# First feed-forward product of the last batch and of all last tokens by Strassen's scheme, seven products of 256x128x512 for eight

## The chip, the cores and the metric

The kernel runs on one core of one Trainium2 chip. The metric is the device time of one execution in microseconds (us), median of three runs. Five engines work side by side and meet at semaphores: PE (the matrix engine, with PEld for its weight loads), DVE (vector), ACT (scalar), POOL and SP (which issues most transfers).

## What is computed

Block-causal attention over 8 batches, 8 heads, 576 tokens, 64 columns a head, then a feed-forward layer with a maximum over three products, all in float32:

```python
B, H, S, D = attn_out.shape
x = attn_out.transpose(0, 2, 1, 3).reshape(B * S, H * D)      # 4608 x 512
h = np.maximum(np.maximum(x @ w1, x @ w2), x @ w3)            # 4608 x 768
return (h @ w_out).astype(np.float32)                         # 4608 x 512
```

## The kernel before

Channels (512, in four tiles of 128 that belong to the four pairs of heads) lie on the partitions and tokens on the free axis. Each float32 operand of the feed-forward products is split into a float32r high part and a float32r rest, and a product is three matmuls: high by high, high by rest, rest by high (`Chunk.product`, L1381). The split of an activation is a cast on ACT (`high`, printed as L286) and a subtraction on POOL (`low`, L291); L286, L288 and L291 are lines of the helpers `copy` and `minus`, which many steps share.

A batch has 576 tokens: 512 go through the feed-forward layer as one `Chunk` (L1317) of 512 columns. The last 64 tokens of each batch are stored to a scratch tensor `rest` in HBM (`Pair.save`, L1236); after the last batch the 8 x 64 of them are loaded back and split (`Rest`, L1261) and make one more chunk of 512 columns. A `Chunk` makes 6 tiles f of 128 hidden columns; for each, the three weights i and the four channel tiles c give 12 steps of three matmuls of 128x128 by 128x512, so 216 matmuls, into a PSUM bank `pm` for each (f, i). ACT copies the bank of i = 0 to SBUF (`m`), DVE takes the maximum with the other two (`most`, L1400), ACT and POOL split the result into `hh`, `hl`. Then four output tiles tt of 128 tokens take 6 x 3 matmuls each (`project`, L1415), 72 in all; ACT copies the bank (`get`) and SP sends it off (`put`, L1430).

The order on every engine is written by a planner (`in_order`, L65). Each step is a job with a cost for each engine, a rank, the jobs that it waits for and the buffers ("slots") that it takes and gives. The planner plays the program through with these costs; a free engine takes the ready job of the lowest rank (`NOW` is the lowest of all), and the order that comes out is the order in which the instructions stand in the engines' queues. The products of the chunk of batch b-1 fill PE between the attention of batch b, so that after the attention of batch 7 there remain, in this order: the rest of batch 6's products, its projections, the products and projections of batch 7's 512 tokens, and the products and projections of the last tokens (L1476 to L1490).

The weights are split once at the start and stay in SBUF as `wh`, `wl` (tiles `w0` to `w17`).

Of the kernel before, what the change touches and what calls it, by code (L numbers as in the profile page):

```python
# [9 lines left out]
F32 = mybir.dt.float32  # L10
# [24 lines left out]
LOAD = 520.0  # L35
# [115 lines left out]
def pe(*cols, least=128):  # L151
    return sum(max(n, least) / 2.4 + 13.5 for n in cols)


def dve(n, fast=False):
    return (70.0 if fast else 72.0) + n / (1.92 if fast else 0.96)


def act(n, psum=True):
    return (55.0 if psum else 95.0) + n / 1.2  # L160


def pool(n):
    return 120.0 + 2.2 * n
# [3 lines left out]
def kernel(  # L168
# [40 lines left out]

    slots = dict(  # L210
        sb=5, sb5=4, scores=4, pm=3, stat=2, stat4=2, p0=2, p1=2, p2=2, p3=2, p4=1,
        x32=2 * XB, x=NP, m=3, qn=2, kn=2, vn=2, kq=2, q8=1, pz=2, pt=2,
    )
    for f in range(NF):
        slots[f"hh{f}"] = slots[f"wo{f}"] = 1
# [58 lines left out]
    def job(cost, rank, call, *args, after=(), take=(), give=(), lasts=0.0, moved=0.0, behind=None, alone=("POOL",)):  # L274
        j = Job(cost, rank, lambda eng: call(eng, *args), after, take, give, lasts, moved, behind, alone)

        j.late = 500.0 if call.__name__ in ("qk4", "block", "pv") else 250.0
        jobs.append(j)
        return j

    def join(after, give):
        return job({}, 0, lambda eng: None, after=after, give=give)

    def copy(eng, dst, src):
        if eng == "ACT":
            nc.scalar.copy(dst, src)  # L286
        else:
            nc.vector.tensor_copy(dst, src)  # L288

    def minus(eng, dst, a, b):  # L290
        {"DVE": nc.vector, "POOL": nc.gpsimd}[eng].tensor_tensor(out=dst, in0=a, in1=b, op=ALU.subtract)  # L291
# [4 lines left out]
    class Unit:  # L296


        def __init__(self, u, src, dst, n, prior, *early):
            self.gate, first = early[0] if 4 <= u < 3 * NF else None, None  # L300
            if u < 4:
                pair, first = made[1 + u if u < 3 else 0], "kn" if u < 3 else "vn"
                self.gate, first = (pair, first), pair.loads[first]
            self.src, self.dst, self.n, self.u = src, dst, n, u
            self.last = n == DO
            rank = DELAY + PACE * u


            self.tag = f"wo{dst}" if self.last else f"w{u}"
            self.temps = SPARE[dst] if self.last else (f"wo{u % NF}",)  # L310
            j = self.issued = job(
                {"POOL": ASK},
                rank - 8,
                self.load,
                alone=(),
                after=(prior and prior.issued, first, *(e.sized for e in early if e)),
                take=(self.tag,) if self.last else (),
            )
            j = job({}, 0, lambda eng: None, after=(j,), lasts=MOVE, moved=2000.0)
            j = self.sized = job({"ACT": act(512, False)}, rank, self.size, after=(j,), take=self.temps)  # L320
            for step, fast in (
                (self.clamp, True),
                (self.shift, True),
                (self.sign, False),
                (self.power, True),
                (self.rest, False),
            ):
                c = dve(512, fast)
                j = job({"DVE": c}, rank, step, after=(j,), take=("m",) if step == self.rest else (), alone=("DVE",))
            rest, j = j, job({"ACT": act(512, False)}, rank, self.high, after=(j,))  # L330
            if u >= APART:
                j = job({"DVE": dve(512)}, rank, self.less, after=(j,))
                join((j,), self.temps)
            j = job(
                {"PE": (2 if u >= APART else 6) * pe(512)},
                rank,
                self.whole,
                after=(j, rest),
                take=("pm",),
                give=("m",) if u >= APART else (*self.temps, "m"),  # L340
            )
            self.done = job({"ACT": act(512)}, rank, self.lower, after=(j,), give=("pm",))

        def load(self, eng):
            st = moe.tile([P, 1024], F32, name=self.tag, bufs=1)
            if self.gate:

                if isinstance(self.gate, Unit):
                    a = self.gate.a
                else:  # L350
                    pair, nm = self.gate
                    a = pair.rows[:, pair.k0] if nm == "kn" else pair.vn[:, 0, 0]
                nc.gpsimd.tensor_copy(st[0:1, 0:1], a[0:1, 0:1])
            st = st.bitcast(I32)
            nc.gpsimd.dma_start(st.rearrange("p (c f) -> p c f", f=2 * self.n), self.src.bitcast(I32))
            lo_hi = st.rearrange("p (n t) -> p n t", t=2)
            self.low_word, self.high_word = lo_hi[:, :, 0].bitcast(U32), lo_hi[:, :, 1]
# [62 lines left out]
        def high(self, eng):  # L420
            w = moe.tile([P, 2, 512], F32R, name=self.tag, bufs=1)
            self.h, self.l = w[:, 0], w[:, 1]
            if self.last:
                woh[self.dst], wol[self.dst] = self.h, self.l
            else:
                wh[self.dst], wl[self.dst] = (t.rearrange("p (c f) -> p c f", f=P) for t in (self.h, self.l))
            copy(eng, self.h, self.a)
# [830 lines left out]
            xh, xl = (self.tokens(t) for t in (self.xs[0].bitcast(F32), self.xs[1]))  # L1258
            minus(eng, xl, self.firsts(), xh)

    class Rest:  # L1261


        def __init__(self, c, first, prior):
            self.c, self.prior = c, prior
            fresh = c in (0, 3)
            j = job(
                {"SP": LOAD},
                first,
                self.load,  # L1270
                after=(saved[c], made[-1].ended, prior and prior.loaded),
                take=("pz",) if fresh else (),
                lasts=LOAD + DMA,
            )
            self.loaded = j
            j = self.highs = job(
                {"ACT": act(512, False)},
                first,
                self.high,
                after=(j, prior and prior.highs),  # L1280
                take=(("pt",) if c == 0 else ("p3",)) if fresh else (),
            )
            self.xjob = job(
                {"POOL": pool(512)},
                first,
                self.low,
                after=(j, prior and prior.xjob),
                take=(("pt",) if c == 0 else ("p3",)) if fresh else (),
            )

        def room(self, nm, dtype):
            if self.c == 0 or (self.c == 3 and nm == "pz"):
                return att.tile([P, 4 * RUN], dtype, name=nm, bufs=2)
            return att.tile([P, 512], dtype, name="p3", bufs=slots["p3"])

        def part(self, t):
            return t[:, 512 * (self.c % 3) :][:, 0:512]

        def load(self, eng):
            self.z = self.room("pz", F32) if self.c in (0, 3) else self.prior.z  # L1300
            nc.sync.dma_start(self.part(self.z), rests[self.c])

        def high(self, eng):
            t = self.h = self.room("pt", F32R) if self.c in (0, 3) else self.prior.h
            self.xs = [self.part(t)]
            copy(eng, self.xs[0], self.part(self.z))

        def low(self, eng):
            t = self.l = self.room("pt", F32R) if self.c in (0, 3) else self.prior.l
            self.xs.append(self.part(t))  # L1310
            minus(eng, self.xs[1], self.part(self.z), self.xs[0].bitcast(F32))

    NOW = -1.0e3

    class Chunk:  # L1317
# [112 lines left out]
                queue.dma_start(out[a : a + n, :], ob[p0 : p0 + n, :])  # L1430


    chunks, made = [], []

    def plan(b, part, gap):
# [8 lines left out]
    def tiles(b, *ts):  # L1444
        return [((b * S + P * t, 0, P),) for t in ts]
# [28 lines left out]
        start, before = rank + END, pairs  # L1474
    made[-2].alone(rank - 8)
    made[-1].alone(rank + SECOND)  # L1476
    end = start + PAIR * NP * 2 / 3
    chunks.append((slice(0, 512), tiles(B - 1, 3, 2, 0, 1), before, start, end))
    rest = None
    ends = [rest := Rest(c, rank + SECOND + 2 * PAIR + c, rest) for c in range(NP)]  # L1480
    own = [tuple((b * S + 512, 64 * (b % 2), 64) for b in (2 * tt, 2 * tt + 1)) for tt in range(B // 2)]
    chunks.append((slice(0, 512), own, ends, end, end + PAIR * NP * 2 / 3))
    weights()
    for unit in units.values():
        unit.done.next.append(cleared[0])
# [2 lines left out]
    prior = None  # L1488
    for rows, ts, pairs, start, end in chunks:
        prior = Chunk(rows, ts, pairs, prior, start, end)  # L1490
    with tc.manual_schedule(engines=None):
        for j, eng in in_order(jobs, slots):
            j.call(eng)
# [30 lines left out]
```

## Time and profile before

| what | us |
|---|---|
| median of 3 runs | 858.4 |
| lowest and highest run | 858.19, 858.67 |
| span of the profiled execution, first to last instruction | 856.2 |
| median above the span of the profiled execution | 2.2 |
| last instruction of attention on PE ends, from the span's start | 699.4 |
| batch 6's projections end | 720.7 |
| last matmul ends | 851.8 |

The profile is of one execution. Times in it count from the first instruction. Engines work at once, so busy shares do not add to a time; the chain that ended last is followed back from the last instruction and is what has to get shorter. A duration of one matmul is from its start to its end, and neighbours overlap, so the pace of a row of matmuls is read from the length of a stretch and their count.

### The profile page before, as it was taken

To read this page: it belongs to the slowest core of one execution; us is meant where nothing else is said; L and a number is where in the kernel's file an instruction comes from. 1 tells how busy PE (TensorE), PEld (TensorE's weight loads), DVE (VectorE), ACT (ScalarE), POOL (GpSimd) and SP (SyncE) were. 2 spreads that over 40 slices of the span, in tenths; PEclk is the share of its full clock that TensorE was granted. 3 is DMA by queue.
4 is the path that set the end of the run, shared out by engine and by line. 5 is a ranking of instruction groups with operands and counts; after the bars stand their busy time and mean duration, and the time that the engine had idled before them with its cause. 6 is when DMAs were issued, how large, how long until landed. Compare 5 with 4: busy or idle time off the path is not lost.

```text
span 856.2 us, 14915 instructions
## 1 busy us (share of the span) xinstructions
PE 845.7 (99%) x4862; PEld 673.4 (79%) x4862; DVE 518.2 (61%) x1524; ACT 468.2 (55%) x1318; POOL 302.1 (35%) x342
## 2 busy tenths in 40 slices
PE   8999999999999999999999999999999999999998
PEld 6577877878877788788878787888788778888886
DVE  6999997868872876568664866386638710110110
ACT  5998867757771775546573657455665422111111
POOL 3352122554353354514461345234443323110110
PEclk9999999999999999999999999999999999999999
DMA  8765358684777276745583558456655441001002
GB/s 242 220 185 143 69 104 186 137 190 90 158 166 177 49 155 145 158 104 111 112 192 76 112 118 172 118 117 124 131 144 109 93 116 64 0 1 50 0 1 50
DMA packets 240974, 100.36 MB, mean 117 GB/s; under 512 B 203008, under 2 KB 232704, under 8 KB 240896
## 3 DMA queue, kind: packets, MB, share of 16 engines
q1 hardware_dynamic: 236272, 86.42, 46.5%
q0 software_dynamic: 3456, 12.58, 4.5%
q8 instruction: 39, 0.64, 0.3%
q10 hardware_dynamic: 1168, 0.39, 0.2%
q14 instruction: 39, 0.32, 0.1%
HBM read 42.99 MB, written 10.49 MB: 62 GB/s over the span
## 4 chain that ended last, share of the span: by engine, by line
PE 88%; ACT 5%; DVE 3%; DMA 2%; issue 1%; SPq 0%; ACTq 0%; DVEq 0%
PE pm L1386 49%; PE pm L1415 16%; PE pm L1217 7%; PE sb L1025 6%; PE sb L1217 3%; PE sb L1155 2%; PE sb L1143 1%; ACT p L677 1%; DMA pt<-pz 1%; ACT w L286 1%; PE pm L416 1%; DMA wo<-in_moe_w_out_dram 1%; DVE sb L493 1%; DVE pz L700 1%; ACT p L509 0%
## 5 line engine op out<-in xcount | busy, mean ns | idle before, releaser
L1386 PE MATMUL pm<-xh,w 128*128 128x512 f32 (+1 forms) x1296 | 385.9, 371 | 0.5 <-DVE m L1400 0.5
L1386 PEld LDWEIGHTS pm<-xh,w 128*128 128x128 f32 x1296 | 237.0, 188 | 46.6 <-issue 5.1
L1386 PE MATMUL pm<-xl,w 128*128 128x512 f32 (+1 forms) x648 | 237.1, 366 | 0.0
L677 ACT ACTIVATE p<-sb,nm 128x512 f32<-128x512 f32 (+3 forms) x256 | 133.8, 529 | 100.2 <-DVE nm L493 98.4
L1400 DVE TENSOR_TENSOR m<-pm,m 128x512 f32<-128x512 f32 (+1 forms) x120 | 74.5, 621 | 138.8 <-PE pm L1386 138.5
L700 DVE STREAM_TRANSPOSE pz<-p 128x512 f32<-128x512 f32 (+1 forms) x280 | 133.8, 523 | 24.7 <-POOL p L513 11.8
L291 POOL TENSOR_TENSOR hl<-m,hh 128x512 fp32r<-128x512 f32 (+1 forms) x60 | 72.8, 1213 | 203.2 <-ACT hh L286 202.8
L493 DVE CUSTOM_DVE_ANT_1 sb<-sb,mask 128x256 f32<-128x256 f32 (+2 forms) x224 | 120.7, 567 | 36.5 <-PE sb L1155 34.9
L1386 PEld LDWEIGHTS pm<-xl,w 128*128 128x128 f32 x648 | 122.1, 188 | 19.5 <-issue 1.2
L1415 PE MATMUL pm<-wo,hh 128*128 128x512 f32 x432 | 134.4, 392 | 0.0
L291 POOL TENSOR_TENSOR kq<-kq 128x576 fp32r<-128x576 f32 x48 | 68.5, 1436 | 165.0 <-ACT kq L286 165.0
L513 POOL TENSOR_TENSOR p<-p,rs 128x512 f32<-128x512 f32 (+4 forms) x100 | 82.4, 850 | 101.5 <-DVE rs L857 66.4
L286 ACT CAST hh<-m 128x512 fp32r<-128x512 f32 (+1 forms) x60 | 34.7, 578 | 133.1 <-DVE m L1400 132.9
L286 ACT COPY m<-pm 128x512 f32<-128x512 f32 (+1 forms) x96 | 53.7, 560 | 96.4 <-PE pm L1415 64.8
L1415 PEld LDWEIGHTS pm<-wo,hh 128*128 128x128 f32 x432 | 80.3, 188 | 17.3 <-issue 0.8
L509 ACT ACTIVATE p<-p,rs 128x128 f32<-128x128 f32 (+4 forms) x173 | 87.7, 567 | 9.4 <-DVE rs L857 6.5
L1415 PE MATMUL pm<-wo,hl 128*128 128x512 f32 x216 | 84.1, 389 | 0.0
L1217 PE MATMUL pm<-pt,vn 128*64 128x320 f32 (+4 forms) x616 | 64.4, 360 | 0.0
L1217 PEld LDWEIGHTS pm<-pt,vn 128*64 128x64 f32 x616 | 38.5, 137 | 24.7 <-issue 1.8
L1025 PEld LDWEIGHTS sb<-kq 64*128 64x128 f32 x576 | 47.8, 185 | 8.6 <-issue 7.4
L1025 PE MATMUL sb<-kq 64*128 64x384 f32 (+3 forms) x576 | 53.0, 325 | 0.0
L677 ACT ACTIVATION_READ_ACCUMULATOR p<-sb,nm 128x1 f32 x256 | 51.6, 201 | 0.0
(130 smaller groups left out, 967.2 us busy)
## 6 DMA issues: line engine op xcount, KB each, us to landing
pt<-pz SPq DMA_DIRECT2D x224, 200.0 KB, 3.8
w<-in_moe_w_dram POOLq DMA_DIRECT2D x18, 512.0 KB, 5.7
vn<-in_v_dram SPq DMA_DIRECT2D x64, 128.0 KB, 3.5
out_dram<-m SPq DMA_DIRECT2D x32, 256.0 KB, 2.1
kq<-in_k_dram SPq DMA_DIRECT2D x112, 72.0 KB, 2.4
kq<-in_q_dram SPq DMA_DIRECT2D x112, 72.0 KB, 2.4
wo<-in_moe_w_out_dram POOLq DMA_DIRECT2D x6, 512.0 KB, 4.0
kq<-in_k_dram SPq DMA_DIRECT2D x8, 128.0 KB, 5.2
```

What stands on the lines that cost most here:

```text
L286: nc.scalar.copy(dst, src)
L291: {"DVE": nc.vector, "POOL": nc.gpsimd}[eng].tensor_tensor(out=dst, in0=a, in1=b, op=ALU.subtract)
L493: nc.vector.tensor_tensor_reduce(out=ps, in0=ps, in1=hidden, scale=-SCALE, scalar=first, op0=ALU.add, op1=ALU.min, accum_out=out_)
L509: nc.scalar.mul(p, p, r)
L513: nc.gpsimd.tensor_tensor(out=p, in0=p, in1=r.broadcast_to([P, p.shape[1]]), op=ALU.mult)
L677: nc.scalar.activation(dst, src, AF.Exp, bias=nm[:, c : c + 1], scale=-1.0, accum_out=sm[:, c : c + 1])
L700: nc.vector.transpose(dst, p[:, 0 : n * P])
L1025: nc.tensor.matmul(h.ps[t], qs[h.own, P * t : P * (t + 1)], ks[h.own, 0 : P * (t + 1)], start=(n == 0), stop=(n == 2),)
L1217: nc.tensor.matmul(o[h.own].rearrange("p (i u) -> p i u", u=n)[:, :, c0 : c0 + z - a], self.vn[own, kt, h.j, :], h.pt[own, :, h.off + a : ...
L1386: nc.tensor.matmul(self.ps, w[i, f][:, c, :], xx, start=(c == 0 and s == 0), stop=(c == NC - 1 and s == 2))
L1400: nc.vector.tensor_tensor(out=m, in0=ps, in1=m, op=ALU.max)
L1415: nc.tensor.matmul(self.po, h, w[f], start=(f == 0 and s == 0), stop=(f == NF - 1 and s == 2))
```

## The change

Let X be the 512 tokens of batch 7 and Z the 512 last tokens, each with its upper and lower half of channels (two tiles of 128), and let (u, v) be two hidden tiles of the same weight i. Four blocks of weights by four blocks of activations are a 2x2 block product of eight products of 256x128x512 (six matmuls each). For each of the nine groups g = (i, pair of f) the change makes it with seven, numbered 1 to 7, by the Winograd form of Strassen's scheme. `Twin` takes the place of `Rest` and of the last two `Chunk`s.

- On the activations' side it makes t1 = Z_up - X_up, t2 = Z_low - t1, t3 = Z_low - Z_up and t4 = X_low - t2 for both tiles of a half (`sums`), and splits these and Z_low ("b") into high and rest, once.
- On the weights' side each group adds high and rest of its four blocks (`whole`), makes four sums (`mix`) and splits them (`mix_cut`, two pieces of 512 columns) into buffers that the hidden tiles `hh2` to `hh5` of the chunk before have left.
- On the outputs' side products share banks: 1, 6, 7 and 4 add up in one, 5 and 3 in another, 2 has its own. ACT copies the bank after 1, 6 and 5 (`keep`: p1, u2, p5) before the next product may add to it, and DVE adds such a copy to a bank for three of the four outputs of a group and takes the maximum over i (`out`): c11 and c21 are hidden tiles u and v of batch 7, c12 and c22 those of the last tokens.
- The order of products is 1 and 2 of group 0, and then for each group 6, 1 of the next, 5, 7, 2 of the next, 3, 4.
- The eight output tiles are projected after all products, f = 4 and 5 of the first two tiles behind f = 0 to 3 of both.

The core of the diff (helpers that only place buffers are left out):

```diff
-        x32=2 * XB, x=NP, m=3, qn=2, kn=2, vn=2, kq=2, q8=1, pz=2, pt=2,
+        x32=2 * XB, x=NP, m=3, qn=2, kn=2, vn=2, kq=2, q8=1, pz=2, pt=2, sf=1,
...
-    class Rest:
...
+    class Twin:
...
+        ORDER = (6, "1", 5, 7, "2", 3, 4)
...
+            for c in (0, 2, 1, 3):
+                loads.append(
+                    job(
+                        {"SP": LOAD},
+                        start - 8,
+                        self.fetch,
+                        c,
+                        after=(saved[c], made[-1].later, *loads[-1:]),
+                        take=("kq",) if c in (0, 1) else (),
+                        lasts=LOAD + DMA,
+                    )
...
+            for j in range(2):
+                used += self.sums(j, z[j], z[2 + j], start - 6 + j)
...
+            order = [(0, 1), (0, 2)]
+            for g in range(NG):
+                order += [(g + 1, int(p)) if isinstance(p, str) else (g, p) for p in self.ORDER]
+            self.made, self.ms, done = {}, {}, {}
+            last, n = prior.last, 0
+            for g, p in order:
+                if g == NG:
+                    continue
+                if p == 1:
+                    self.begin(g, start + step * n)
+                last = done[g, p] = self.product_job(g, p, start + step * n, last, one, done)
...
+            turns = [(tt, f) for tt in (0, 1) for f in range(4)] + [(tt, f) for tt in (0, 1) for f in (4, 5)]
+            turns += [(tt, f) for tt in range(2, len(tiles)) for f in range(NF)]
...
+            t1 = job({"DVE": 2 * dve(512)}, r, self.add1, j, after=(z0, x0, *(h.moved for h in made[-1].heads)), take=("sb",))
+            h1, l1 = split("t1", t1, r, "DVE")
+            t2 = job({"DVE": dve(512)}, r, self.add2, j, after=(t1, z2), take=("sb",))
+            join((t2, l1), ("sb",))
+            h2, l2 = split("t2", t2, r, "DVE")
+            t3 = job({"POOL": pool(512)}, r, self.add3, j, after=(t1, z2))
+            split("t3", t3, r, "POOL", psum=False)
+            t4 = job({"DVE": 2 * dve(512)}, r, self.add4, j, after=(l2, x2))
+            split("t4", t4, r, "DVE", give=("sb",))
+            b = join((z2, t1), ())
+            split("b", b, r, "POOL", psum=False)
...
+        def add1(self, eng, j):
+            t = self.t["t1", j] = psa.tile([P, 512], F32, name="sb")
+            xh, xl = (u.bitcast(F32) for u in self.x[j].xs)
+            minus("DVE", t, self.z[j], xh)
...
+        def begin(self, g, rank):
+            u, v = self.units_of(g)
+            after = (units[u].done, units[v].done, *(x.moved for x in made[-1].heads))
+            two = () if g == 7 else ("hh4", "hh5") if g % 2 == 0 else ("hh2", "hh3")
+            whole = job({"DVE": 4 * dve(256)}, rank - 9, self.whole, g, after=after, take=("p1", "p1", "p2", "p2"))
+            s = job({"DVE": 4 * dve(256)}, rank - 9, self.mix, g, after=(whole,), take=("sf",), give=("p1", "p1", "p2", "p2"))
+            lows = []
+            for n in range(2):
+                h = job({"ACT": act(512, False)}, rank - 8, self.mix_cut, g, n, 0, after=(s, self.prior.projected, *lows), take=() if n else two)
+                lows.append(job({"POOL": pool(512)}, rank - 8, self.mix_cut, g, n, 1, after=(h, *lows)))
+            join(lows, ("sf",))
...
+            a11, a12, a21, a22 = self.w4
+            nc.vector.tensor_tensor(out=s1, in0=a21, in1=a22, op=ALU.add)
+            minus("DVE", s2, s1, a11)
+            minus("DVE", s3, a11, a21)
+            minus("DVE", s4, a12, s2)
...
+            if p in (5, 6):
+                need.append(self.ready["s", g][0])
+            if p in (7, 3):
+                need.append(self.ready["s", g][1])
+            held = {6: "p1", 7: "u2", 3: "p5", 4: "c22"}.get(p)
+            if held:
+                need.append(self.made[g, held])
+            if p in (1, 2):
+                need += [units[u].done for u in self.units_of(g)]
...
+            if p in (1, 6, 5):
+                nm = {1: "p1", 6: "u2", 5: "p5"}[p]
+                free = self.made.get((g - 1, {1: "c11", 6: "c12", 5: "c22"}[p]))
+                self.made[g, nm] = job({"ACT": act(512)}, NOW, self.keep, g, key, nm, after=(j, free), take=room)
+            outs = {2: ("c11", "p1"), 3: ("c12", "u2"), 7: ("c22", "p5"), 4: ("c21", None)}.get(p)
+            if outs:
+                self.out_job(g, key, *outs, j, p)
...
+            cost = {"ACT": act(512)} if i == 0 and nm is None else {"DVE": dve(512) * (2 if i and nm else 1)}
...
+            if i == 2:
+                room = () if side else (f"hh{f}",)
+                h = job({"ACT": act(512, False)}, NOW, self.high, f, side, c, after=(o,), take=room)
+                e = "DVE" if g == 8 and side == 0 else "POOL"
+                l = job({e: dve(512) if e == "DVE" else pool(512)}, NOW, self.low, f, side, c, after=(h,), give=(slot,))
...
+            if p in (1, 2):
+                ws = [[w[u][:, 2 * (p - 1) + c, :] for w in (wh, wl)] for c in range(2)]
+                xs = [self.x[2 * (p - 1) + c].xs for c in range(2)]
+            elif p == 4:
+                ws = [[w[v][:, 2 + c, :] for w in (wh, wl)] for c in range(2)]
+                xs = [[self.t["t4", c, k] for k in range(2)] for c in range(2)]
+            else:
+                n = (5, 6, 7, 3).index(p)
+                ws = [
+                    [self.t["s", g, n // 2, k][:, 256 * (n % 2) + P * c :][:, 0:P] for k in range(2)] for c in range(2)
+                ]
+                nm = ("t1", "t2", "t3", "b")[n]
+                xs = [[self.t[nm, c, k] for k in range(2)] for c in range(2)]
+            for c in range(2):
+                (h, l), (xh, xl) = ws[c], xs[c]
+                for s, (w, x) in enumerate(((h, xh), (h, xl), (l, xh))):
+                    nc.tensor.matmul(
+                        self.banks[g, key],
+                        w,
+                        x,
+                        start=(p in (1, 2, 5) and c == 0 and s == 0),
+                        stop=(c == 1 and s == 2),
+                        skip_group_check=True,
+                    )
...
+            t = self.temp(g, "t") if i else m
+            nc.vector.tensor_tensor(out=t, in0=ps, in1=self.temp(g, nm), op=ALU.add)
+            if i:
+                nc.vector.tensor_tensor(out=m, in0=t, in1=m, op=ALU.max)
...
-    end = start + PAIR * NP * 2 / 3
-    chunks.append((slice(0, 512), tiles(B - 1, 3, 2, 0, 1), before, start, end))
-    rest = None
-    ends = [rest := Rest(c, rank + SECOND + 2 * PAIR + c, rest) for c in range(NP)]
-    chunks.append((slice(0, 512), own, ends, end, end + PAIR * NP * 2 / 3))
+    twin = before, tiles(B - 1, 3, 2, 0, 1) + own, start, start + PAIR * NP * 4 / 3
...
+    Twin(twin[0], twin[1], prior, *twin[2:])
```

## Rows read from the trace of the kernel before

**Rows 1.** The page's head: busy time, share and instructions by engine; chain by engine.

```profile
PE 845.7 (99%) x4862; PEld 673.4 (79%) x4862; DVE 518.2 (61%) x1524; ACT 468.2 (55%) x1318; POOL 302.1 (35%) x342
...
PE 88%; ACT 5%; DVE 3%; DMA 2%; issue 1%; SPq 0%; ACTq 0%; DVEq 0%
```

**Rows 2.** The chain that ended last, its end: start us, length us, what.

```profile
696.57 2.86 PE sb L1217 x28
699.42 4.98 PE pm L1386 x21
704.41 16.32 PE pm L1415 x72
720.73 48.96 PE pm L1386 x216
769.69 16.32 PE pm L1415 x72
786.01 49.46 PE pm L1386 x216
835.47 16.38 PE pm L1415 x72
...
851.91 0.59 ACT m L286
```

**Rows 3.** Stretches of the tail: window, length, engines busy us (count), clock, DMA share, GB/s.

```profile
704.41:720.73 16.32, 16.32 (x73) 13.52 (x73) 1.09 (x2) 5.25 (x10) 8.81 (x8) 1.00 0.19 66
720.73:769.69 48.96, 48.96 (x217) 40.55 (x217) 7.61 (x11) 7.22 (x12) 6.44 (x5) 1.00 0.02 6
...
786.01:835.47 49.46, 49.46 (x217) 40.57 (x217) 7.61 (x11) 7.22 (x12) 6.48 (x5) 1.00 0.02 6
```

**Rows 4.** Groups of 720.73 to 835.47: busy us, mean ns | idle before.

```profile
L1400 DVE TENSOR_TENSOR m<-pm,m 128x512 f32<-128x512 f32 x23 | 15.9, 692 | 112.1 <-PE pm L1386 112.1
L291 POOL TENSOR_TENSOR hl<-m,hh 128x512 fp32r<-128x512 f32 x11 | 14.2, 1291 | 101.2 <-ACT hh L286 101.2
...
L286 ACT COPY m<-pm 128x512 f32<-128x512 f32 x17 | 10.0, 587 | 35.4 <-PE pm L1415 16.7 <-PE pm L1386 10.0 <-POOL hl L291 8.6
...
L286 ACT CAST hh<-m 128x512 fp32r<-128x512 f32 x11 | 6.8, 622 | 61.1 <-DVE m L1400 61.1
```

**Rows 5.** DVE by shape, whole span: additions of 256 and 512 columns.

```profile
L1400 DVE TENSOR_TENSOR m<-pm,m 128x256 f32<-128x256 f32 x24 | 9.9, 412 | 2.0 <-PE pm L1386 2.0
...
L291 DVE TENSOR_TENSOR w<-wo,w 128x512 fp32r<-128x512 f32 x7 | 4.9, 706 | 0.6 <-ACT w L286 0.6
```

**Rows 6.** Line 403, two SBUF inputs: durations min/median/max; timeline around the longest.

```profile
L403 DVE SCALAR_TENSOR_TENSOR m<-w,wo x18: 675/684/692, 21.7 to 85.9; 128x512 fp32r<-128x512 uint32 x18
...
117.45 1.14 POOL L513 TENSOR_TENSOR p<-p,rs 128x576 f32<-128x576 f32 x1 [8.23 <-DVE rs L1204]
...
117.51 1.63 DVE L403 SCALAR_TENSOR_TENSOR m<-wo,pz 128x512 fp32r<-128x512 uint32 x1
```

**Rows 7.** Timeline of 704 to 714: the last pair's tokens on their way back.

```profile
705.05 0.48 DVE L288 COPY x<-sb 128x320 f32<-128x320 f32 x1
...
709.58 0.37 SPq L1301 DMA_DIRECT2D pz<-rest  x1
...
712.49 0.62 ACT L286 CAST p<-pz 128x512 fp32r<-128x512 f32 x1 [3.37 <-DMA pz<-rest]
```

**Rows 8.** Timeline: ACT back to back, the end of batch 6's projections, a split.

```profile
705.17 0.62 ACT L286 CAST hh<-m 128x512 fp32r<-128x512 f32 x1 [1.47 <-DVE m L1400]
705.70 0.61 ACT L286 CAST xh<-x 128x512 fp32r<-128x512 f32 x1
...
720.81 0.59 ACT L286 COPY m<-pm 128x512 f32<-128x512 f32 x1 [3.48 <-PE pm L1415]
...
836.23 0.62 ACT L286 CAST hh<-m 128x512 fp32r<-128x512 f32 x1 [5.58 <-DVE m L1400]
...
836.99 1.29 POOL L291 TENSOR_TENSOR hl<-m,hh 128x512 fp32r<-128x512 f32 x1 [6.93 <-ACT hh L286]
```

More of the change, by code (lines that the diff above doesn't have):

```diff
@@ L1259, in x_low @@
             minus(eng, xl, self.firsts(), xh)
-    class Rest:
[L1264 to L1311, printed above, removed]
     NOW = -1.0e3
```

213 lines of the change are left out of this document (added).

## The prediction, made before the change was run

> **What bounds the kernel now.** I read the page's head first, for which engine could set the time at all: PE is busy for 845.7 of 856.2 us, the next engine (DVE) for 61%, and PE carries 88% of the chain that ended last [rows 1]. Then the end of the chain in order of time, since the change lies there: from the last attention matmul (699.42) to the copy behind the last matmul (851.91) there are only matmuls, one block after the other with no idle piece between them [rows 2]. Then the stretches of that tail by engine: over batch 7's products PE is busy for all 48.96 us at granted clock 1.00, DVE for 7.61, ACT for 7.22, POOL for 6.44; over the last tokens' products much the same; over batch 6's projections (704.41 to 720.73) DVE for 1.09, ACT for 5.25 and POOL for 8.81 of 16.32 [rows 3]. So in the tail the time is the number of matmuls times their pace, and the other engines have room; last, the rows of the groups, for what one step on them costs [rows 4, 5]. What I must find out is whether they have enough room, and at the right moments.
>
> **Matmuls.** Removed: two blocks of 216, 48.96 + 49.46 = 98.42 us, which is 226.7 ns a matmul in the first and 229.0 in the second [rows 2]. The first reads the activations where batch 7's pairs left them, the second reads split tiles in reused attention buffers. Added: 9 groups x 7 products x 6 matmuls = 378 of the same shape. The 9 x 2 x 6 = 108 of products 1 and 2 read batch 7's activations as they are (226.7), and the 270 others read sums in reused buffers, nearest to the second block (229.0): 24.48 + 61.83 = 86.31. Saved: **12.1 us**; with all 378 at 226.7 it would be 12.7, all at 229.0 11.9. The 144 projection matmuls stay (16.32 + 16.38 [rows 2]), only their order changes, and the way from the last matmul to the end is the same: one copy and one store.
>
> **Sums of activations.** For each of two tiles: t1 and t4 take two DVE additions each, t2 one, the rests of t1, t2 and t4 one each: 8, so 16 in all of about 0.70 us (0.692 with one bank as input, 0.706 with both in SBUF [rows 4, 5]), 11.2 us. ACT has 10 casts of 0.62, 6.2 us; POOL has t3 and the rests of t3 and b, 6 of 1.29, 7.7 us [rows 4]. `Rest`'s four casts and four subtractions go. All of this fits beside batch 6's projections (16.32 us with DVE at 1.09 [rows 3]), if the data is there. What comes last is the last pair's tokens: its output is copied from 705.05, the load back is issued at 709.58, and ACT starts on it at 712.49 [rows 7]. From there t2 of the second tile needs addition, cast, addition: 2.0 us and hops; if all 5.6 us of the first tile's DVE work stood in front, it would be 7.7, so 714.6 to 720.2. The first product that reads it, 6 of group 0, comes 12 matmuls (2.72) behind the projections, at 723.4. Cost on the path: nothing, with 3 to 9 us to spare. On SP only these four loads move, from one buffer to another; batch 6's stores stand among them as before.
>
> **Start of group 0.** The new wait here is that `mix_cut` may not write `hh4` before batch 6's last projection has read it (720.73). Behind that projection ACT first copies out its bank (starts 720.81; neighbours on ACT start 0.53 apart: 705.17 and 705.70), then casts (0.62), then POOL subtracts (1.29, starting 0.14 behind the cast's end: 836.23 + 0.62 to 836.99) [rows 8]: 720.81 + 0.53 + 0.62 + 0.14 + 1.29 = 723.4, and a hop of 0.1 to 0.2 to PE, its first weight load behind it. PE wants it at 723.4, since only products 1 and 2 (2.72) cover it. I take a stall of 0.3 us; between 0, if the hop is hidden, and 1.6, if one POOL subtraction of another step stands in front.
>
> **Each group.** Weights: 8 DVE additions of 256 columns of 0.41 (3.3 us), 2 casts, 2 POOL subtractions (2.6 us). Outputs: 7 DVE steps of 0.69 (4.8; for i = 0 only 3), 3 ACT copies of 0.59, and every third group 4 splits [rows 4, 5]. A group with i > 0 thus takes 8.1 us of DVE and, with its share of splits (4/3), 4.3 of POOL under 42 matmuls or 9.6 us of PE. No engine is over its time in sum. What counts is the distance between a bank's reader and the next product in that bank: `keep` after 6 and after 5 has two products in between (2.73 us) for one ACT copy of 0.59; c22 after 7 has two products for an addition and a maximum on DVE, 1.4 us and 0.3 of hops, so 1.0 to spare. Queued in front of c22 on DVE can be a block of four 0.41 additions of the next group (1.65). Behind c22 stand c11 of the next group and c12, and for c22 waits PE itself (product 4). So c22 is the one place in a group where PE can come to stand. I take 0.1 us for each of the seven groups behind the second, 0.7 in all; the ends are 0 and the two rivals below.
>
> POOL and DVE may hinder each other: a DVE step with two SBUF inputs that takes 0.68 at the median took 1.63 when it began 0.06 behind a POOL multiplication of 1.14 [rows 6]: it seems to have waited out POOL. Additions with a bank as one input took 0.692 beside POOL's work of the same stretch [rows 4]. Of a group's DVE steps the 8 weight additions and 3 maxima have both inputs in SBUF, 5.4 us, and POOL has 4.3: if they exclude each other, 9.7 us under 9.6 of PE, and the room is gone. The Trainium skill, "SBUF — State Buffer", section "Who interferes with whom", states just this: a vector instruction with two SBUF inputs and a GpSimd instruction that reads SBUF take a shared read port, the first to issue keeps it for its whole length, the other fully blocks. The stretched step agrees. By that rule rival 1 gains, and the sum would be its 854.3 instead of the 847.3 below.
>
> **The end of the products.** c21 of the last group (maximum, cast, rest on DVE: 0.69 + 0.62 + 0.70 and hops, 2.5 us) is hidden by f = 0 to 3 of the first two output tiles, 24 matmuls, 5.4 us; with two POOL steps in the way (2.6) still so. Cost: nothing.
>
> **Sum.** The profiled execution spans 856.2 us and the median is 858.4; I let the 2.2 us between them stand. 856.2 - 12.1 + 0.3 + 0.7 = 845.1 of span, and 858.4 - 11.1 = **847.3** as the median.
>
> **Rivals.**
> 1. *The vector engines set the pace.* Sums of DVE and POOL that exclude each other are as long as PE's group, so that c22 comes one POOL subtraction (1.29) late in each of the six groups with i > 0: 858.4 - 12.1 + 0.3 + 6 x 1.29 = 854.3 (between 850 and 857 by how many groups). For it: the stretched row and the sums above. Against it: the three groups with i = 0 have 3 DVE steps for 7, and let the queue catch up; a wait of PE gives all others time.
> 2. *Slower: c22 behind a weight block and two POOL steps.* If the order on DVE puts a block of `mix` (1.65) ahead of c22 and both it and the maximum wait out a POOL subtraction (2 x 1.29), c22 takes 1.65 + 2.58 + 1.4 + 0.3 = 5.9 us where two products give 2.73: 3.2 a group, 19 in the six, and 858.4 - 12.1 + 0.3 + 19 = 865.6. It decides from a mean wait of 12.1 / 9 = 1.35 us a group on. Against it: the planner puts c22's rank ahead of all weight work, and POOL is busy for under half of a group.
> 3. *A late start.* The sums of activations are not ready for product 6 of group 0, because the load back or the splits fall behind other work of ACT or DVE: each us of delay beyond the 3 to 9 to spare shows in full. With 4 us late: 851.3. For it: DVE and ACT carry twice the work there, in one order. Against it: the spare.
> 4. *It doesn't do what it says*: the same number of matmuls, or an order that leaves products of group 0 in front of the projections and so no cover at the start (2.7 more, 850). The counts in the code speak against the first; for the second, product 1 needs the second pair's rest, and the planner has it queued on POOL behind batch 6's last split.
>
> **How the numbers follow.** This kernel's runs lie within 0.06%, so 0.2% (1.7 us) can be told from no change. Forecast, 847.3: 0.72, its own range 845.8 (12.7 saved, no stall) to 849.5 (0.4 us a group). Rival 1: 0.12. Rivals 3 and 4 with a gain left: 0.07. No difference, by any of them near the balance: 0.03. Slower, rival 2: 0.06. Faster then is 0.72 + 0.12 + 0.07 = 0.91. The range reaches to 852.5, which takes in rivals 3 and 4 and a third of rival 1.
>
> **What will show it.** Right: PE's work between 720.7 and the first of the 144 last matmuls lasts 86 to 88 us with 378 matmuls, granted clock 1.00; one short idle stretch at 723.4 with POOL as releaser; PE's other waits name DVE (c22) and stay under 1 us together; the weight sums of group 0 stand before 720 on DVE. Wrong: idle PE in each group released by DVE, maxima of well over 0.7 us beside POOL steps (rival 1, 2), a wait of several us before product 6 (rival 3), or a granted clock below 1.00 in the tail, which no row of the tail shows now and for which I have no price.

## The result and the profile after

| | before | after |
|---|---|---|
| median, us (4 runs each) | 858.3 | 850.0 |
| lowest to highest | 857.61 to 858.67 | 849.36 to 850.47 |
| span of the profiled execution | 856.2 | 847.5 |
| tail: batch 6's projections end to last matmul's end | 131.1 | 123.2 |

The ratio is 0.9908, with a 95% interval of 0.9894 to 0.9922: 8.3 us saved where 11.1 were forecast. The tail of the profiled execution is 7.9 us shorter. The other 0.8 of span was gained before 260 us, where PE has the same work; nothing there belongs to the change. (Over the runs below the products start between 719.3 and 721.2, so a difference of 1 us between two runs is read from the length of the products and not from the median alone.) In the listing of the kernel after, `Twin.product` is L1667, `project` L1721, `whole` L1546, the first step of `mix` L1554, the addition of `out` L1695 and its maximum L1697.

The chain that ended last, beside [rows 2] (start, length, what; parts left out):

```profile
703.58 16.32 PE pm L1361 x72
719.90 1.36 PE sb L1667 x6
721.26 1.36 PE pm L1667 x6
722.62 5.56 PE sb L1667 x24
...
737.99 2.18 DVE p L1546 x3
740.17 0.61 DVE hl L1695
740.78 0.04 issue
740.83 7.21 PE sb L1667 x30
...
777.98 2.93 DVE p L1546 x2
780.92 0.61 DVE w L1695
781.53 0.04 issue
781.57 7.18 PE sb L1667 x30
788.76 1.38 PE pm L1667 x6
790.13 0.58 ACT w L286
790.71 0.04 issue
790.76 8.60 PE sb L1667 x36
799.36 1.36 PE pm L1667 x6
800.72 8.29 PE sb L1667 x36
809.01 0.68 PE pm L1721 x3
809.69 1.40 PE sb L1667 x6
811.09 32.02 PE pm L1721 x141
```

Where [rows 2] had matmuls only, DVE now stands in the chain: weight additions (L1546), then one addition of `out` (L1695), then PE with product 4; once it is a copy on ACT, and PE with product 3 behind it. The products last from 719.90 to 811.09 less the 0.68 of a projection that slipped in between: 90.5 us for 378 matmuls. With them goes PE's list of waits in the tail (rows of other engines left out; us in total, times, longest; a wait shows partly at the weight load PEld and partly at PE):

```profile
PEld sb L1667 <- DVE w L1695: 2.2, 2, 1.4
...
PEld sb L1667 <- ACT w L286: 1.4, 2, 1.1
PE sb L1667 <- DVE w L1695: 1.4, 2, 1.0
...
PEld sb L1667 <- DVE hl L1695: 0.7, 1, 0.7
...
PE sb L1667 <- ACT w L286: 0.6, 1, 0.6
...
PE sb L1667 <- DVE hl L1695: 0.3, 1, 0.3
```

From the starts of neighbouring matmuls the waits are 0.5 (product 4 of group 1), 0.2 (7 of 3), 0.6 (4 of 4), 1.3 (4 of 5) and 0.9 us (3 of 6), 3.6 in all: 2.4 before product 4, which waits for c22, and 1.1 before products 7 and 3, which wait for ACT's copies. The steps that stand in the chain have three sorts of duration (ns, min/median/max):

```profile
L1546 DVE TENSOR_TENSOR p<-w x36: 407/416/1521, 693.0 to 779.4; 128x256 f32<-128x256 f32 x36
L1697 DVE TENSOR_TENSOR m<-w,m x10: 692/693/1740, 742.1 to 810.0; 128x512 f32<-128x512 f32 x10
L1695 DVE TENSOR_TENSOR w<-sb,w x10: 673/692/692, 748.1 to 809.3; 128x512 f32<-128x512 f32 x10
```

The additions with a bank as one input (L1695) never take more than 0.69; those with two SBUF inputs take up to 1.1 us more than alone. The longest wait shows why (timeline of 774 to 782.5, DVE and then POOL):

```profile
777.31 3.60 DVE L1546 TENSOR_TENSOR p<-w 128x256 f32<-128x256 f32 x4
780.84 0.68 DVE L1695 TENSOR_TENSOR w<-sb,w 128x512 f32<-128x512 f32 x1
...
777.71 2.92 POOL L291 TENSOR_TENSOR w<-kq,w 128x512 fp32r<-128x512 f32 x2 [1.27 <-ACT w L286]
```

Four additions that take 1.4 us by themselves (as at 763.5 in the same trace) took 3.6, while POOL made two rests; c22 of group 5 stood behind them, and product 4 began 0.04 us behind c22's addition (781.53 to 781.57), not behind its maximum. Ahead of these four stood, without a pause, the four steps of `mix`: eight weight additions in a row, 774.9 to 780.9, and in the same way ahead of product 4 of groups 1 (735.3 to 740.2) and 4 (765.3 to 770.0). Through groups 4 and 5 DVE had hardly a pause (windows: length, then PE, PEld, DVE, ACT and POOL busy, granted clock, DMA share, GB/s):

```profile
768.00:778.30 10.30, 9.94 (x44) 7.83 (x43) 9.96 (x17) 3.32 (x6) 3.10 (x3) 1.00 0.00 0
778.30:789.00 10.70, 9.67 (x42) 7.61 (x42) 10.49 (x12) 2.25 (x4) 6.75 (x5) 1.00 0.00 0
```

So two readings have to be told apart: that stretched steps stand in the wrong place of DVE's queue, and that DVE has, with the stretch, as much work as time.

### The profile page after: what moved, and what is told of

The parts are those of the page before. It is cut to its first block, busy times and chain, and to the rows that moved or that the text cites. A ratio compares the mean times of both kernels' runs of the same rounds, so it can differ in the third digit from the quotient of the medians.

```text
span 847.5 us, 15017 instructions
## 1 busy us (share of the span) xinstructions
PE 835.3 (99%) x4808; PEld 662.3 (78%) x4808; DVE 591.9 (70%) x1641; ACT 490.5 (58%) x1360; POOL 327.9 (39%) x360
## 4 chain that ended last, share of the span: by engine, by line
PE 85%; DVE 8%; ACT 5%; issue 1%; DMA 0%; ACTq 0%; DVEq 0%
PE pm L1332 39%; PE pm L1361 13%; PE pm L1217 7%; PE sb L1025 6%; PE sb L1667 5%; PE pm L1721 4%; PE sb L1217 3%; PE sb L1155 2%; DVE p L1546 2%; PE sb L1143 1%; ACT p L677 1%; ACT w L286 1%; DVE kq L291 1%; DVE sb L493 1%; PE pm L416 1%
## 5 line engine op out<-in xcount | busy, mean ns | idle before, releaser
L1332 PE MATMUL pm<-xh,w 128*128 128x512 f32 (+1 forms) x1152 | 341.4, 368 | 0.3 <-DVE m L1346 0.3
L1332 PEld LDWEIGHTS pm<-xh,w 128*128 128x128 f32 x1152 | 209.9, 188 | 40.9 <-issue 5.3
L1332 PE MATMUL pm<-xl,w 128*128 128x512 f32 (+1 forms) x576 | 209.2, 363 | 0.0
L291 POOL TENSOR_TENSOR kq<-kq 128x576 fp32r<-128x576 f32 (+1 forms) x50 | 71.1, 1429 | 165.2 <-ACT kq L286 159.6
L1332 PEld LDWEIGHTS pm<-xl,w 128*128 128x128 f32 x576 | 108.6, 188 | 16.7 <-issue 1.2
L1361 PE MATMUL pm<-wo,hh 128*128 128x512 f32 x336 | 104.8, 393 | 0.0
L509 ACT ACTIVATE p<-p,rs 128x128 f32<-128x128 f32 (+4 forms) x173 | 87.7, 568 | 9.4 <-DVE rs L857 6.4
L1361 PEld LDWEIGHTS pm<-wo,hh 128*128 128x128 f32 x336 | 62.2, 188 | 13.6 <-issue 0.8
L1346 DVE TENSOR_TENSOR m<-pm,m 128x512 f32<-128x512 f32 (+1 forms) x96 | 57.8, 603 | 19.2 <-PE pm L1332 18.8
L1361 PE MATMUL pm<-wo,hl 128*128 128x512 f32 x168 | 65.4, 389 | 0.0
L1025 PE MATMUL sb<-kq 64*128 64x256 f32 (+3 forms) x576 | 52.7, 325 | 0.0
```

The costliest lines, as they stand in the source:

```text
L509: nc.scalar.mul(p, p, r)
L1025: nc.tensor.matmul(h.ps[t], qs[h.own, P * t : P * (t + 1)], ks[h.own, 0 : P * (t + 1)], start=(n == 0), stop=(n == 2),)
L1332: nc.tensor.matmul(self.ps, w[i, f][:, c, :], xx, start=(c == 0 and s == 0), stop=(c == NC - 1 and s == 2))
L1346: nc.vector.tensor_tensor(out=m, in0=ps, in1=m, op=ALU.max)
L1361: nc.tensor.matmul(self.po, h, w[f], start=(f == 0 and s == 0), stop=(f == NF - 1 and s == 2))
```

## Experiments

Two theories. **A**: DVE steps with two SBUF inputs wait out POOL's subtractions, and that makes c22, or a copy that PE needs, late. **B**: DVE's order alone, with weight additions ahead of c22, is too late whatever POOL does. Each experiment starts from the changed kernel. Over all runs the kernel before took 857.1 to 859.6 us, so medians of four runs that lie within 1 us of each other are not told apart.

**e1, POOL writes in place of reading.** Each rest on POOL becomes:

```diff
-                minus(eng, t, src, self.t["s", g, n, 0].bitcast(F32))
+                h = self.t["s", g, n, 0].bitcast(F32)
+                minus(eng, t[:, 0:1], src[:, 0:1], h[:, 0:1])
+                for _ in range(2):
+                    nc.gpsimd.memset(t.bitcast(F32), 0.0)
+                minus(eng, t[:, 0:1], src[:, 0:1], h[:, 0:1])
```

> POOL's rests of weight sums and of hidden tiles are left out: each subtraction of 512 columns becomes a one-column subtraction, two memsets of 512 columns and a one-column subtraction, of about the same length in all, at the same place of POOL's queue and with the same waits, but reading almost nothing from SBUF (the rests are then zero). DVE, ACT and PE keep all their work. Theory A (DVE steps with two SBUF inputs wait out POOL's subtractions, and that puts c22 and the copy of bank 5 late): additions of 256 columns all near 0.41 us (now up to 1.52), PE idle between the products under 0.8 us in all (now 3.8), median about 3 us below the changed kernel's 850.0: 846.5 to 847.5. Theory B (the order on DVE alone, c22 behind eight weight additions, is too late whatever POOL does): additions still near 0.41 in the gaps, but PE stands idle before product 4 as now; 849.5 to 850.5.

Measured: 846.55 us, ratio 0.9863 (0.9848 to 0.9877). PE has no wait between the products. `whole` (L1546) and the first step of `mix` (L1554) in the changed kernel (groups between 719 and 812: busy us, mean ns | idle before):

```profile
L1546 DVE TENSOR_TENSOR p<-w 128x256 f32<-128x256 f32 x28 | 17.3, 675 | 0.0
...
L1554 DVE TENSOR_TENSOR kq<-p,p 128x256 f32<-128x256 f32 x8 | 7.5, 932 | 0.6 <-DVE p L1546 0.5
```

`whole` and POOL in e1:

```profile
L1546 DVE TENSOR_TENSOR p<-w 128x256 f32<-128x256 f32 x28 | 10.0, 419 | 0.0
...
L1574 POOL MEMSET hl<- 128x512 f32 x32 | 16.8, 526 | 1.9
L291 POOL TENSOR_TENSOR hl<-kq,hh 128x1 fp32r<-128x1 f32 x32 | 6.7, 213 | 25.8 <-ACT hh L286 24.6
```

A rest takes 2 x 0.526 + 2 x 0.213 = 1.48 us, no less than before, and DVE's queue is as long; yet the 28 additions fall from 675 to 419 ns. It is POOL's subtractions that stretched them (e1 takes away their reading and the kind of instruction together, and does not tell the two apart). That decides for A. It also gives the matmul term by itself: the products run from 720.23 to 807.81 less 0.68, 86.9 us without a wait.

**e2, more cover for c22.** Product 4 goes behind product 6 of the next group:

```diff
-        ORDER = (6, "1", 5, 7, "2", 3, 4)
+        ORDER = ((0, 6), (-1, 4), (1, 1), (0, 5), (0, 7), (1, 2), (0, 3))
```

> One change: product 4 of a group comes one product later, behind product 6 of the next group, so that c22 has three products of cover (4.1 us) for two (2.7). Theory A and B both: the three waits before product 4 (0.5, 0.6 and 1.3 us) go, the stretched DVE steps stay; 847.3 to 848.3, and what stays is the wait of 0.9 before product 3 of group 6. If the stalls come from the sum of work on DVE and not from where c22 stands, they move to other products and the time stays 849.5 to 850.5.

Measured: 851.6 us, ratio 0.9921 (0.9906 to 0.9936): no gain, where both theories had 847.3 to 848.3. The median is 1.6 us above the changed kernel's, but the two intervals overlap, and the products take 91.0 us for 90.5. The waits before product 4 are gone, as both theories had it, but 4.1 us of others came, the longest before product 3 of group 6 (timeline around 790: DVE, POOL, ACT, PE):

```profile
787.44 1.51 DVE L291 TENSOR_TENSOR kq<-p,p 128x256 f32<-128x256 f32 x1
788.87 1.51 DVE L291 TENSOR_TENSOR kq<-p,kq 128x256 f32<-128x256 f32 x1
790.30 0.68 DVE L1696 TENSOR_TENSOR m<-pm,w 128x512 f32<-128x512 f32 x1
...
787.19 2.90 POOL L291 TENSOR_TENSOR hl<-m,hh 128x512 fp32r<-128x512 f32 x2
...
791.07 1.07 ACT L286 COPY w<-sb 128x512 f32<-128x512 f32 x2 [3.73 <-DVE m L1696]
...
792.20 0.50 PE L1668 MATMUL sb<-vn,hh 128*128 128x512 f32 x1 [2.26 <-ACT w L286]
```

Read from the bottom: product 3 waits for ACT's copy of product 5; that copy is the second of two and stands in ACT's queue behind the copy of product 1 of the next group; that one may not overwrite p1 before c11 (L1696) has read it; and c11 stands behind weight sums that POOL stretched from 0.42 to 1.51. More cover in one place left the cause and moved the wait. The 0.9 us before product 3 of group 6 in the changed kernel come in a like way: there ACT's queue is held by the cast of a hidden tile, which waits for c21's maximum behind stretched steps of `mix`.

**e5, the order of e2 with POOL as in e1** (both diffs).

> Product 4 one product later as in e2 (which measured 851.6, with PE waiting 2.4 us before product 3 of group 6), and POOL's rests of weight sums and hidden tiles left out as in e1 (one-column subtractions and memsets in their place). Theory A (e2's waits too come from DVE's two-input steps that wait out POOL: c11 stands behind stretched weight sums, ACT's copy of product 1 waits for c11, and the copy of product 5 stands behind it): no wait of PE left, 846.2 to 847.3, like e1. If the order of e2 is bad in itself: 849 or more, with waits before product 3.

Measured: 846.4 us, ratio 0.9855 (0.9838 to 0.9873), no wait of PE. e2's waits too go when POOL's reading goes; the order alone does not make them.

**e3, weight additions behind the outputs.** `whole` of group g also waits for c21 of group g-2:

```diff
-            after = (units[u].done, units[v].done, *(x.moved for x in made[-1].heads))
+            after = (units[u].done, units[v].done, *(x.moved for x in made[-1].heads), self.made.get((g - 2, "c21")))
```

> One change: the four additions of high and rest for group g (whole) wait for c21 of group g-2, so that on DVE they stand behind the outputs and not between mix and c22. Theory A: c22 is no longer behind additions that wait out POOL; the waits before product 4 shrink from 2.4 to under 0.8 us in all, 847.5 to 848.7. Theory that only POOL's own lateness matters (sums too late for products 6 and 7): no gain or a loss, 849.5 to 851, with waits before product 6.

Measured: 846.9 us, ratio 0.9866 (0.9851 to 0.9881); as e10 on another chip 846.45, 0.9861 (0.9844 to 0.9877). It computes all that the changed kernel does, and is some 3 us faster than it. A said 847.5 to 848.7: the gain was larger. PE's waits come to 0.5 us, and yet DVE is still stretched (groups between 719 and 812):

```profile
L1546 DVE TENSOR_TENSOR p<-w 128x256 f32<-128x256 f32 x28 | 15.8, 625 | 0.0
L1697 DVE TENSOR_TENSOR m<-w,m 128x512 f32<-128x512 f32 x10 | 9.6, 962 | 0.3
...
L1554 DVE TENSOR_TENSOR kq<-p,p 128x256 f32<-128x256 f32 x8 | 3.7, 462 | 0.6
```

For `whole`, 625 ns for 675 is nearly the same stretch as in the changed kernel, and behind the outputs it costs next to nothing. But the new order also took `mix` out of POOL's way (462 ns for 932), so e3 lowers DVE's work as well as moving it, and does not by itself tell place from sum; e7 below does better.

**e4, e2 and e3 together.**

> Both changes together. Theory A: hardly a wait of PE is left between the products (under 0.8 us), 846.5 to 847.5, as fast as with POOL's reads left out. If more cover only moves the stalls: 849 or more.

Measured: 847.5 us, ratio 0.9871 (0.9855 to 0.9888), waits of 0.8. No better than e3 alone.

**e6 and e7, longer POOL work.** Half a subtraction more behind each rest of the weight sums, in the changed kernel (e6) and in e3's (e7):

```diff
                 minus(eng, t, src, self.t["s", g, n, 0].bitcast(F32))
+                minus(eng, t[:, 0:256], src[:, 0:256], self.t["s", g, n, 0].bitcast(F32)[:, 0:256])
```

> The changed kernel, with half a subtraction more (256 columns, the same values again) behind each of the 18 rests of weight sums on POOL: 0.65 us each, 1.3 a group. Theory A: DVE's two-input steps wait longer, PE's idle time between the products grows from 3.8 to 6 to 11 us; 852 to 857. If POOL's reads don't matter: within 0.5 of 850.0.

> The same longer POOL work in the kernel of e3, where the additions of high and rest stand behind c21 on DVE (846.9). If what decides is that stretched steps stand ahead of c22 and c11, most of it stays hidden: 847 to 849. If e3 only had room for so much: 850 to 855.

Measured: e6 858.25 us, ratio 0.9995 (0.9985 to 1.0004), so the whole gain is gone, somewhat more than A had expected; e7 848.85, 0.9886 (0.9871 to 0.9902), as A expected. The same POOL work costs 8.2 us in one place of DVE's additions and some 2 in the other. Part of e6's profiled execution is a second price (windows: length, PE, PEld, DVE, ACT, POOL, granted clock, DMA, GB/s; then PE's timeline at its longest wait):

```profile
739.00:749.00 10.00, 7.09 (x20) 5.25 (x19) 8.89 (x14) 1.53 (x4) 3.85 (x3) 0.66 0.00 0
789.00:799.00 10.00, 9.02 (x33) 7.28 (x34) 8.74 (x11) 3.91 (x8) 5.32 (x5) 0.83 0.00 0
```

```profile
742.83 0.79 PE L1668 MATMUL sb<-pz,w 128*128 128x512 f32 x1 [2.90 <-DVE hl L1696]
...
748.11 0.63 PE L1668 MATMUL sb<-xh,w 128*128 128x512 f32 x1
748.54 0.58 PE L1668 MATMUL sb<-xl,w 128*128 128x512 f32 x1
748.95 0.62 PE L1668 MATMUL sb<-xh,w 128*128 128x512 f32 x2
```

Behind waits of 2.9 and 2.8 us the granted clock of the stretch falls to 0.66 and 0.83 and matmuls start 0.43 us apart for 0.23: the lower of the two levels, 1.2 GHz for 2.4, over 14 and 8 matmuls, 4.3 us together. Behind the wait of 1.7 us of the same run matmuls stayed 0.23 apart. Not every execution paid that much: the mean granted clock of e6's ten runs lies between 0.993 (the profiled one among them) and 1.000, and the run at 1.000 took 858.0 us all the same.

The profiled executions side by side (products: first to last, less the 0.68 of the projection in between; waits: above e1, or above e5 for the order of e2; DVE: the 78 steps among the products that have both inputs in SBUF; the 32 with a bank as one input take 22 us in every run):

| | products, us | waits, us | DVE's two-input steps, us |
|---|---|---|---|
| changed kernel | 90.5 | 3.6 | 54.9 |
| e1 | 86.9 | 0 | 37.8 |
| e2 | 91.0 | 4.1 | 50.9 |
| e3 | 87.4 | 0.5 | 48.2 |
| e4 | 87.7 | 0.8 | 46.0 |
| e5 | 86.9 | 0 | 37.7 |
| e6 | 100.1 | 13.2, of which 4.3 by the clock | 62.0 |
| e7 | 89.5 | 2.6 | 54.0 |

Place counts: e7 has as much two-input work as the changed kernel and waits 1.0 us less, and e2 has 4.0 us less of it and waits more. The sum may count too: e1, e3, e4 and e5, which wait least, are those that have least of it. How e3's gain divides between the two stays open.

**e8, the pace.** All products take the batch's own activations as moving operand, so the sums are made for nothing:

```diff
+            xs = [self.x[c].xs for c in range(2)]
             for c in range(2):
                 (h, l), (xh, xl) = ws[c], xs[c]
```

> A look at the pace: in the changed kernel all seven products read the split activations of batch 7's first two pairs as moving operand, in place of the sums (which are still made and split). If the place of the moving operand sets the pace of 230 to 234 ns of products 4 to 7, all products run at 226.7 to 228 and the 378 matmuls shrink by 0.5 to 1 us; if it is the stationary operand (fresh sums for products 3, 5, 6, 7) or the switch between them, products 5 to 7 stay at 230 or more.

Measured: 849.4 us in a single run; PE's waits grew to 4.1 us, while the pace of all 378 matmuls fell from 230.1 to 227.1 ns, 1.1 us in all. The 24 matmuls from product 6 of group 0 on take 5.44 us (226.7 ns each), where the changed kernel takes 5.56 (231.7): it is the moving operands that make products 4 to 7 slower. Product 1 tells that it is not a tile's place alone: it reads the same tiles in both runs, and behind product 6 takes 230 ns a matmul in the changed kernel and 226.7 in e8.

**e9, addresses.** e3 with pz, pt and p3 moved by 64 bytes, through the sizes of small statistics tiles:

```diff
-att.tile([P, 2, NT], F32, name=nm, bufs=slots["stat"])
+att.tile([P, 2, NT + 4 * (nm == "rs")], F32, name=nm, bufs=slots["stat"])
...
-                self.stat = tuple(
-                    att.tile([P, NT], F32, name=f"{nm}4", bufs=slots["stat4"]) for nm in ("nm", "sm", "rs")
-                )
+                stat = att.tile([P, 3, NT], F32, name="stat4", bufs=slots["stat4"])
+                self.stat = tuple(stat[:, n] for n in range(3))
```

> The kernel of e3 with nothing but addresses moved: four small statistics tiles are made wider or put together, so that one of the two pz buffers, both pt buffers and both p3 buffers begin at a multiple of 128 bytes of their partition where they began 64 bytes behind one (the other pz buffer goes the other way). In e8 all products that read the batch's own tiles, which begin at such a multiple, ran at 226.7 ns a matmul; the sums in pz, pt and p3 cost 230 to 234. If the address of the moving operand decides: products 4 to 7 go to 226.7 to 228 ns, the 378 matmuls shrink by 0.6 to 1.0 us, 845.7 to 846.5, and attention may gain by its own reads of pt. If not: as the repeat of e3 on the same chip, within 0.4 us.

> The kernel of e3 once more, on the chip and among the rounds of e9, for the comparison: 846.5 to 847.4.

Measured: e9 847.3 us, ratio 0.9870 (0.9855 to 0.9885); e10 846.45 as above; the intervals overlap. The medians differ by 0.85 where 0.4 was expected, but the products take 87.6 and 87.5 us, so the difference lies ahead of them. A row of products without a wait takes 8.30 us for 36 matmuls in e9 and 8.29 in e10: to begin at a multiple of 128 bytes does not cure it. Addresses are not ruled out, since single products did change: product 2, whose tiles e9 leaves where they were, took 231.0 ns a matmul for 227.3, product 5 233.2 for 230.6, product 1 228.1 for 230.0. Why products 1 and 4 to 7 take 230 to 233 ns a matmul, and products 2 and 3 about 227 to 228, stays open; up to 1.2 us hang on it (378 x 226.7 = 85.7 for 86.9).

## Why the prediction was right in direction and range and short in size

- **What bounds the kernel, and the matmul term: right but for 0.6 us.** In e1, with nothing to wait for, 378 matmuls take 86.9 us where 98.4 went, so 11.5 saved for the 12.1 forecast: the forecast had 86.3, and products 4 to 7 and product 1 take 230 ns and more, not the 229.0 and 226.7 taken from [rows 2]. That e1's medians give 12.1 as well (858.6 to 846.55) is chance.
- **Sums of activations: nothing on the path, right.** The last of them ends on POOL at 718.2, 4.2 us ahead of product 6 of group 0.
- **Start of group 0: 0.3 forecast, nothing measured.** Product 6 began without a gap (timeline: ACT, POOL, PE):

```profile
719.98 0.59 ACT L286 COPY m<-pm 128x512 f32<-128x512 f32 x1 [3.05 <-issue]
720.46 0.62 ACT L286 CAST hh<-kq 128x512 fp32r<-128x512 f32 x1
...
721.16 2.61 POOL L291 TENSOR_TENSOR hl<-kq,hh 128x512 fp32r<-128x512 f32 x2 [2.95 <-ACT hh L286]
...
722.46 0.63 PE L1667 MATMUL sb<-pt,hh 128*128 128x512 f32 x2
```

  The copy, the cast and the subtraction follow each other as summed up from [rows 8], to 722.45. But a product's first two matmuls read the high part alone; the rest is wanted at the third, 0.46 us later. I had let it be wanted at the first. e4 shows it: the one wait of PE there, for a rest on POOL, stands before the third matmul of product 6 of group 7.
- **Each group: the failed step.** "I take 0.1 us for each of the seven groups behind the second, 0.7 in all": it is 3.6. The place was right for 2.4 of it: c22. The size was not. I let four additions stand ahead of c22 and priced them at 1.65, though [rows 6] stood beside it: eight stood there in a row, and with POOL's subtractions in the way the last four of them alone took 2.5 (group 1) and 3.6 (group 5). That PE waits for c22's addition alone and not for the maximum gave 0.7 back. The other 1.1 came before products 7 and 3: ACT's copies were priced as free with two products of cover, without what stands ahead of them in ACT's queue.
- **The rivals.** The truth lies between the forecast and rival 1: 850.0 is above the forecast's own range, which ended at 849.5, and at the lower edge of rival 1's 850 to 857 (by its own sum, six groups give at most 854.3). Only the wider range to 852.5, which took in a part of rival 1, holds it. What happened is rival 1's mechanism, in five places and not in every group with i > 0. [rows 6] was read as a total (9.7 us under 9.6, the room is gone); that came true for some 20 us, where DVE had no pause (20.45 of 21.00), and for the rest of the groups not. The total does not settle it by itself: nearly as much two-input work costs 3.6 us in the changed kernel and 2.6 in e7. Waits near rival 2's size (3.2) came about in e6 alone, twice, and there with a loss of clock that had no price. By the rule of the Trainium skill, "SBUF — State Buffer", section "Who interferes with whom", a GpSimd instruction that only writes does not contend with DVE's second input; e1 agrees, with 419 for 675 ns.
- **The end of the products: right.** From the last product on, 141 matmuls follow without a gap (811.09, 32.02).
- **The sum.** In the tail 120.0 us were forecast (131.1 - 12.1 + 1.0) and 123.2 came: 2.6 more of waits, 0.6 of pace. The median's 850.0 is 2.7 above the forecast for the same reasons. The spread of 0.06% that the prediction went by was that of three runs; over all runs of the kernel before it is 0.3%.

## What to carry to other kernels

Where a matrix engine's time is bought with sums on other engines, find the step of them that it waits for in each round, and price that step with everything that can stand ahead of it in its queue, stretched by whatever may hold it up; the sums of work per engine alone say too little. A step with slack belongs behind the ones that are waited for, and a dependency that is not needed for the data can put it there; here the change that did so gave 3 us, part of it perhaps because the new order also met less of POOL's work. When a wait has a cause upstream, more cover in one place moves it: look for what is late, not for who waits.

## What the runs showed of the hardware

- A DVE addition with two SBUF inputs of 0.42 us took up to 1.52 while POOL subtracted in SBUF, and 0.42 while POOL wrote only; with a bank as one input it stayed at 0.69 throughout. POOL's subtractions of 1.29 us ([rows 4]) took up to 1.74 among such steps.
- PE at granted clock 1.00 fell to the lower level behind single waits of 2.9 and 2.8 us (e6), for 14 and 8 matmuls, and stayed at the upper behind 1.7 (e6) and 2.3 (e2).
- Matmuls of one shape ran at 227 or at 230 to 233 ns a piece by their moving operands, and the same tiles gave both paces (product 1 in e8 and in the changed kernel, product 2 in e9 and e10); a start 64 bytes off did not decide it, and the cause is open.
